# Low parts of two output-projection chunks moved from VectorE to GpSimd, and a planner that counts on later first loads

## The chip, the cores and the metric

The kernel runs on one core of one Trainium2 chip. The metric is device time in microseconds (us) of one execution; the time before is the median of three. The engines are TensorE (PE; PEld is its weight load), VectorE (DVE), ScalarE (ACT) and GpSimd (POOL). SyncE (SP) issues every DMA of the kernel, in one queue. SBUF is the memory on the chip that all engines read, PSUM the accumulators (eight banks) that TensorE writes.

## What is computed

Two independent halves share one output of 2048 rows: 448 columns from a Fourier mixing (A) and 448 from attention with 16 heads of width 28 (B).

```python
a = einsum("bsd,ed->bse", x, dft_hid_re); b = einsum("bsd,ed->bse", x, dft_hid_im)
A = einsum("ts,bse->bte", dft_seq_re, a) - einsum("ts,bse->bte", dft_seq_im, b)
q, k, v = split_heads(x @ wqkv)                      # S = 2048, D = 448, H = 16
p = softmax(einsum("bhqd,bhkd->bhqk", q, k) * Dh ** -0.5)
B = merge_heads(einsum("bhqk,bhkd->bhqd", p, v)) @ wo
out = concatenate([A, B], axis=-1)
```

All is float32. TensorE multiplies in a reduced form of it, so most operands are split: a high part (a ScalarE copy into that form) and a low part (the original less the high part, a subtraction on VectorE or GpSimd), and a product takes three matmuls: high by high, low by high, high by low.

## The kernel before

**Work and its order.** Every operation is a task with a key (a due time), the engines that may run it, an estimated duration and the tiles it uses. `Schedule.run` plays the program through once with these estimates and emits each engine's instructions in the order that comes out. On the chip that order is fixed: each engine and the sync queue takes its own list strictly in turn, and waits at an instruction until what it reads is there and what it overwrites has been read. For a load the planner counts a landing time (L274), which for loads planned between T_IN - 6 = 14 us and 45 us has 1.5 us on top.

**The attention.** A unit is one head by 512 queries. In most units ("kept", `unit_kept`) TensorE makes the scores once (L809), ScalarE copies them from PSUM to SBUF (L416), and VectorE takes the running maximum (L816, L819). A chain of small VectorE operations turns that into a shift per query (L824 to L842), which ends in a PSUM bank; ScalarE copies it to SBUF (`mb`, L844). Then eight pairs of tiles are shifted (L859, 128x1024: on VectorE with the shift read from PSUM, or on GpSimd with the shift from `mb`; the first three pairs of a unit, and all pairs of the last units, may go to either) and exponentiated on ScalarE (L863). Eighteen units ("twice", `unit_twice`) make the scores a second time instead, with the maximum as two rows of the product (L755, L759, then L787), and ScalarE exponentiates straight from PSUM (L791). Both end in products with V in two groups of sixteen matmul records (L736), accumulated in one bank and copied to a tile `ou` (L416 on ScalarE or L418 on VectorE).

**Normalising.** `out_of` folds `ou` (L878), copies the result to SBUF (L880), and takes the sums through DRAM: a store-and-load into `sm` (L883), a reciprocal on VectorE (L884), a store to `rd` (L885), a load that spreads it (L889), a product on GpSimd (L892) and the store of the attention output to `ond` (L895). For the last two heads this is done per chunk of 512 queries.

**The output projection**, at the end, per chunk `n` of 512 queries in the order 0, 1, 3, 2: four loads of the attention output from `ond` (L952, and L957 twice for the last 64 rows, which hang on the last two heads). For each half chunk (256 columns) and each of the four pieces `k`, ScalarE makes the high part in a tile of the `k` pool (L970), and a subtraction the low part. The subtraction is recorded in the helper `sub`, so it shows as L412: 128x256, for the last piece 64x256; eight for a chunk. With `early` it goes to VectorE, otherwise to GpSimd. Then TensorE makes four output tiles a chunk, eleven matmuls each (L988), which are copied (L416 or L418) and stored (L995).

**The Fourier half and the weights** fill TensorE's gaps all through: L548 (projections of Q and K, V, and the hidden transform) and L663 (the sequence transform) with pieces of weights that are loaded (L516), copied to a high part on ScalarE (L517) and subtracted to a low part on GpSimd (L523, L532). Q and K go to a DRAM tensor `qkd` (L593, L594), V to `vd` (L620), and come back per head and unit (L690 and L691 for `k` and `q`, L708 for `v`).

Of the kernel before, what the change touches and what calls it, by code (L numbers as in the profile page):

```python
# [39 lines left out]
GV = 8  # L40

TWICE = [(1, 3) if h in (4, 10) else (1,) for h in range(H - 2)] + [(3,), (3,)]
OUT_DVE = True

LAST = (0, 1, 3, 2)

# [124 lines left out]
class Schedule:  # L171
# [34 lines left out]
    def run(self):  # L206
# [10 lines left out]
        while True:  # L217
            for e in self.ENGINES:
                if not idle[e]:
                    continue  # L220
                aside, pick, first = [], None, None
                if e == "SP" and len(landed) >= LANES and landed[-LANES] > now + 1e-9:
                    heapq.heappush(events, (landed[-LANES], 2, count, "tick", None))
                    continue
                heap = self.ready[e]
                before = now - (AHEAD if e == "PE" else 0.0) + 1e-9
                while heap:
                    item = heapq.heappop(heap)
                    t = item[2]
                    if t.n in done:  # L230
                        continue
                    wants = {}
                    for s in t.use:
                        if s.i is None:
                            wants.setdefault(s.pool, []).append(s)
                    if t.since > before or any(not p.can_take(w, before, now) for p, w in wants.items()) or any(
                            x.lock > now + 1e-9 for x in t.lock):
                        aside.append(item)
                        continue
                    if e == "PE" and mode == 1 and t.mode == 0 and pick is None:  # L240
                        if not any(x[2].mode == 1 and x[2].n not in done for x in heap):
                            pick = t
                            break
                        first = first or item
                        aside.append(item)
                        continue
                    pick = t
                    break
                if pick is None and first:
                    pick = first[2]  # L250
                    aside.remove(first)
                for item in aside:
                    heapq.heappush(heap, item)
                if pick is None:
                    continue
                t = pick
                done.add(t.n)
                for s in t.use:
                    if s.i is None:
                        s.pool.take(s)  # L260
                dur = t.engs[e]
                if e == "PE":
                    if t.mode > mode:
                        dur += PE_TURN
                    mode = t.mode
                lat = t.lat
                if e == "SP":

                    at = now
                    for size, extra in t.dmas:  # L270
                        if len(landed) >= LANES:
                            at = max(at, landed[-LANES])
                        flow = max(flow, at + 0.4) + size / (FLOW if now > T_IN else FLOW_IN)
                        landed.append(max(at + 1.35 + size / 170 + extra + (1.5 if T_IN - 6 < now < 45 else 0.0), flow + 1.1))  # L274
                        at += 0.38
                    dur = at - now
                    lat = max(landed[-len(t.dmas):]) - at + 0.1
                t.emit(e)
                count += 1
                idle[e] = False  # L280
                for x in t.lock:
                    x.lock = now + dur + 0.05
                heapq.heappush(events, (now + dur, 0, t.n, "free", (e, t)))
                heapq.heappush(events, (now + dur + t.own, 1, t.n, "own", (e, t)))
                heapq.heappush(events, (now + dur + lat, 1, t.n, "seen", (e, t)))
                if t.lock:
                    heapq.heappush(events, (now + dur + 0.06, 2, t.n, "tick", None))
# [31 lines left out]
def tile_kernel(ctx, tc, xa, wre, wim, wd, xb, wqkv, wo, out):  # L319
# [624 lines left out]
    for n, c in enumerate(LAST):  # L944
# [15 lines left out]
        for i in range(2):  # L960
            x = [kt_s.slot() for _ in range(4)]
            ready = []
            for k in range(4):
                raw, ld = raws[k]
                src = lambda raw=raw, i=i: raw.t[:, i * HF:(i + 1) * HF]
                xh, xl = x[k // 2], x[2 + k // 2]
                hi = lambda xh=xh, k=k: xh.t[:, k % 2 * HF:(k % 2 + 1) * HF]
                lo = lambda xl=xl, k=k: xl.t[:, k % 2 * HF:(k % 2 + 1) * HF]
                key = T_OUT + n + i / 2
                a = act(key, lambda hi=hi, src=src: nc.scalar.activation(hi(), src(), AF.Copy), 0.3, deps=[ld], use=[raw.pair, xh])  # L970
                if k < 3:
                    b = sub(key, lo, src, lambda hi=hi: f32(hi()), d=0.35 if OUT_DVE else 0.65, early=OUT_DVE, deps=[a], use=[raw.pair, xh, xl])
                else:
                    b = sub(key, lambda hi=hi: hi()[64:], lambda src=src: src()[64:], lambda hi=hi: f32(hi())[64:], d=0.35 if OUT_DVE else 0.65, early=OUT_DVE,
                            deps=[a], use=[raw.pair, xh, xl])
                ready += [a, b]
            for t in range(2):
                o = bank_s.slot()

                def cols(k, x=x, t=t):  # L980
                    return lambda: x[k // 2].t[:, k % 2 * HF + t * P:k % 2 * HF + (t + 1) * P]
                seq = products(cols, lambda k, cols=cols: cols(4 + k), lambda cols=cols: cols(3),
                               lambda k: (lambda: w_out.h[:, k]), lambda k: (lambda: w_out.l[:, k]))
                key = T_OUT + 5 + (n * 4 + i * 2 + t) * 2.3

                def emit(e, seq=seq, o=o):
                    for n, (x, w) in enumerate(seq):
                        nc.tensor.matmul(o.t[:, :D], x(), w(), start=(n == 0), stop=(n == 10))  # L988
                m = pe(key, emit, n=11, d=M448, deps=[*ready, *wo_ready], use=[o, *x])
                pair = kept_s.slot()  # L990
                oo = Half(pair, 0)
                e = sch.add({"ACT": 0.43, "DVE": 0.53}, key, lambda e, o=o, oo=oo: copy_of(e, oo.t[:, :D], o.t[:, :D]),
                            deps=[m], use=[o, pair])
                r0 = c * CH + i * HF + t * P
                dma(key, lambda oo=oo, r0=r0: nc.sync.dma_start(out[r0:r0 + P, D:], oo.t[:, :D]), deps=[e], use=[pair])  # L995
# [38 lines left out]
```

## Time and profile before

| what | value |
|---|---|
| median of three runs | 1165.0 us (1163.15 to 1166.09) |
| the profiled execution's own time | 1165.2 us |
| its span, first to last instruction | 1163.4 us, mean granted TensorE clock 0.997 |
| VectorE's low parts of the output projection, 128x256 | 24, mean 0.75 us |
| the same, 64x256 | 8, mean 0.55 us |
| GpSimd's idle time by the waits | 85.6 us for `mb` (L844), 81.1 us for weights (L517) |

How to read the rows: a group row of the waits has engine, what is written, line, then whom it waited for, the total in us, how often, and the longest. A stretch row has its bounds and width, then each engine's busy time with the instructions in brackets, the granted clock (1.00 is full), the share of the DMA engines that is busy, and GB/s. A timeline row has start, duration, engine, line, operation, output<-inputs, shapes, how many in a row, and in square brackets the idle time before and what ended it. SPq rows are issues of DMAs on the sync queue. Matmuls overlap, so the step from one start to the next tells TensorE's pace, not the duration of one row.

### The profile page before, as it was taken

The numbers are of one execution on the slowest core, as the hardware profiler recorded it, in microseconds if no ns is written. First come the engines' busy times: TensorE is split into PE (matmuls) and PEld (weight loads), VectorE is DVE, ScalarE is ACT, GpSimd is POOL, SyncE is SP. The second block draws the span as 40 slices with busy tenths as digits, with TensorE's granted clock in tenths as the row PEclk, the third lists the DMA queues.
The fourth block names the chain that finished last, engine by engine and source line by source line (L and its number), as shares of the span: only waits on it lengthen the run. The fifth ranks groups of instructions, "written<-read, shape, count | busy, mean of one in ns | idle before, by whom it ended". The sixth has DMA issues, their size and how long they took to land.

```text
span 1163.4 us, 19480 instructions
## 1 busy us (share of the span) xinstructions
PE 1142.1 (98%) x6076; PEld 775.1 (67%) x6076; DVE 1012.8 (87%) x1800; ACT 1044.8 (90%) x1782; POOL 917.5 (79%) x534
## 2 busy tenths in 40 slices
PE   8999999999999999999999999999999999999898
PEld 6875666566666666676767576667666666766577
DVE  6599989999999899899989898999998999999832
ACT  5269999999999999999999999999998999999742
POOL 3048887899988889889888999899887998988410
PEclk9999999999999999999999999999999999999999
DMA  8883353222323232332333332222323332323452
GB/s 267 189 175 134 113 177 122 75 86 82 103 69 87 69 110 84 92 92 89 90 94 102 95 95 72 79 80 89 113 93 99 104 120 91 95 64 105 151 158 101
DMA packets 111840, 125.17 MB, mean 108 GB/s; under 512 B 49348, under 2 KB 63316, under 8 KB 111736
## 3 DMA queue, kind: packets, MB, share of 16 engines
q1 hardware_dynamic: 111736, 123.93, 35.7%
q8 instruction: 48, 0.79, 0.3%
q14 instruction: 56, 0.46, 0.1%
HBM read 89.99 MB, written 33.76 MB: 106 GB/s over the span
## 4 chain that ended last, share of the span: by engine, by line
PE 84%; DVE 6%; ACT 4%; issue 2%; DMA 2%; POOL 1%; SPq 1%; DVEq 0%; ACTq 0%; POOLq 0%
PE bank L663 27%; PE bank L736 18%; PE bank L809 14%; PE bank L548 9%; PE bank L787 6%; PE bank L755 5%; PE bank L988 3%; DVE rm L819 2%; ACT kept L416 2%; PE bank L878 1%; POOL kept L859 1%; ACT kept L863 1%; DVE k L412 1%; DMA kept<-wqkv 1%; DVE mx L759 1%
## 5 line engine op out<-in xcount | busy, mean ns | idle before, releaser
L859 POOL TENSOR_TENSOR kept<-kept,mb 128x1024 f32<-128x1024 f32 x269 | 641.1, 2405 | 88.4 <-ACT mb L844 85.6
L819 DVE TENSOR_TENSOR rm<-bank,rm 128x512 f32<-128x512 f32 x644 | 441.1, 685 | 53.4 <-ACT kept L416 20.0
L416 ACT ACTIVATE kept<-bank 128x512 f32<-128x512 f32 (+1 forms) x696 | 410.7, 658 | 59.7 <-PE bank L809 34.6
L863 ACT ACTIVATE kept<-kept 128x1024 f32<-128x1024 f32 x354 | 385.1, 1133 | 12.8 <-DVE kept L859 8.7
L663 PE MATMUL bank<-big,whi 128*128 128x448 f32 x1024 | 324.4, 368 | 0.3 <-DVE big L644 0.3
L809 PE MATMUL bank<-q,k 84*128 84x512 f32 x736 | 286.4, 414 | 4.5 <-ACT kept L416 2.7
L523 POOL TENSOR_TENSOR wlo<-wraw,whi 128x512 fp32r<-128x512 f32 (+1 forms) x166 | 204.9, 1236 | 106.8 <-ACT whi L517 81.1
L736 PE MATMUL bank<-kept,v 128*32 128x512 f32 x1940 | 244.2, 598 | 4.3 <-ACT kept L791 4.1
L663 PEld LDWEIGHTS bank<-big,whi 128*128 128x128 f32 x1024 | 194.2, 190 | 31.7 <-issue 5.2
L759 DVE TENSOR_REDUCE mx<-bank 128x1 f32<-128x512 f32 x288 | 194.8, 680 | 12.1 <-PE bank L755 11.0
L809 PEld LDWEIGHTS bank<-q,k 84*128 84x128 f32 x736 | 134.9, 189 | 99.5 <-DVE rm L819 15.3
L663 PE MATMUL bank<-big,wlo 128*128 128x448 f32 x512 | 188.5, 368 | 0.0
L791 ACT ACTIVATE kept<-bank 128x512 f32<-128x512 f32 x262 | 169.3, 669 | 5.3 <-PE bank L787 5.1
L736 PEld LDWEIGHTS bank<-kept,v 128*32 128x32 f32 x1940 | 56.2, 109 | 122.8 <-issue 108.8
L517 ACT ACTIVATE whi<-wraw 128x512 fp32r<-128x512 f32 x167 | 117.4, 704 | 3.2 <-DMA wraw<-wqkv 2.3
L755 PE MATMUL bank<-k,q 84*128 84x512 f32 x288 | 117.8, 412 | 2.2 <-DMA q<-qkd 1.8
L787 PE MATMUL bank<-q,k 86*128 86x512 f32 x288 | 115.8, 409 | 0.7 <-DMA q<-nmd 0.4
L663 PEld LDWEIGHTS bank<-big,wlo 128*128 128x128 f32 x512 | 97.2, 190 | 13.8 <-issue 0.8
L859 DVE TENSOR_TENSOR kept<-kept,bank 128x1024 f32<-128x1024 f32 x85 | 102.3, 1209 | 2.5 <-ACT mb L844 2.1
L548 PE MATMUL bank<-wd,whi 128*128 128x448 f32 x256 | 80.0, 371 | 0.1
L755 PEld LDWEIGHTS bank<-k,q 84*128 84x128 f32 x288 | 54.2, 189 | 31.1 <-issue 6.0
L548 PE MATMUL bank<-big,whi 128*128 128x512 f32 x196 | 70.1, 402 | 3.4 <-DVE big L412 1.3
(82 smaller groups left out, 1094.0 us busy)
## 6 DMA issues: line engine op xcount, KB each, us to landing
wraw<-wre SPq DMA_DIRECT2D x64, 256.0 KB
wraw<-wim SPq DMA_DIRECT2D x64, 256.0 KB
qkd<-wd SPq DMA_DIRECT2D x32, 256.0 KB
wraw<-xa SPq DMA_DIRECT2D x32, 256.0 KB
k<-qkd SPq DMA_DIRECT2D x64, 112.0 KB
q<-qkd SPq DMA_DIRECT2D x64, 112.0 KB
out<-kept SPq DMA_DIRECT2D x32, 224.0 KB
qkd<-kept SPq DMA_DIRECT2D x24, 256.0 KB
```

Source lines behind the costliest of these rows:

```text
L416: nc.scalar.activation(dst, src, AF.Copy)
L523: b = sch.add(e, at, lambda g: eng[g].tensor_tensor(self.lo.t[:, :n], raw.t[:, :n], f32(self.hi.t)[:, :n], op=ALU.subtract), deps=[a], acq ...
L548: nc.tensor.matmul(o.t[:, :cols], w(), x(), start=(i == 0), stop=(i == n - 1))
L663: nc.tensor.matmul(o.t[:, :D], a.t[:, k, :], b[:, q * 4 + k, :], start=(q == 0 and k == 0 and j == 0), stop=(q == 3 and k == 3 and j == 2))
L736: nc.tensor.matmul(o.t[j * VW:(j + 1) * VW, :], VT[h].t[:, kt // 4, j, :], pairs[i // 2].t[:, i % 2, :], start=(kt < 4), stop=(kt >= NT - 4))
L755: m = pe(key, lambda e, o=o, kc=kc, qt=qt: nc.tensor.matmul(o.t, q.t[:KR, qt * P:(qt + 1) * P], KT[h][kc].t[:KR, :], start=True, stop=True ...
L759: ms.append(dve(key - 20, lambda o=o, kc=kc, qt=qt: nc.vector.tensor_reduce(mx.t[:, qt, kc:kc + 1], o.t, axis=AX.X, op=ALU.max), deps=[m], ...
L787: m = pe(key, lambda e, o=o, kt=kt: nc.tensor.matmul(o.t, KT[h][kt // 4].t[:KR + 2, kt % 4 * P:(kt % 4 + 1) * P], q.t[:KR + 2, :], start=T ...
L809: m = pe(key, lambda e, o=o, kt=kt: nc.tensor.matmul(o.t, KT[h][kt // 4].t[:KR, kt % 4 * P:(kt % 4 + 1) * P], q.t[:KR, :], start=True, sto ...
L819: prev = dve(key - 20, lambda o=o: nc.vector.tensor_tensor(rm.t, o.t, rm.t, op=ALU.max), deps=[m, prev], use=[rm, o], lock=[o], own=RAW)
L859: eng[e].tensor_tensor(s.t, s.t, over_pair(pm.t if e == "DVE" else mb.t), op=ALU.add)
L863: es.append(act(key, lambda s=s: nc.scalar.activation(s.t, s.t, AF.Exp, scale=SCALE), 0.96, deps=[sh], use=[s]))
```

## The change

Two constants of the plan and one threshold. `n` is the place of the chunk in the output projection, so with `OUT_DVE = 2` chunks 0 and 1 have their subtractions on GpSimd (planned at 0.65 us instead of 0.35), chunks 2 and 3 on VectorE as before. The planned landing of loads between 14 and 42 us (45 before) has 3.0 us on top instead of 1.5. No operation is added or removed; the orders change where the planner's times do.

```diff
-OUT_DVE = True
+OUT_DVE = 2
...
-    landed.append(max(at + 1.35 + size / 170 + extra + (1.5 if T_IN - 6 < now < 45 else 0.0), flow + 1.1))
+    landed.append(max(at + 1.35 + size / 170 + extra + (3.0 if T_IN - 6 < now < 42 else 0.0), flow + 1.1))
...
 if k < 3:
-    b = sub(key, lo, src, lambda hi=hi: f32(hi()), d=0.35 if OUT_DVE else 0.65, early=OUT_DVE, deps=[a], use=[raw.pair, xh, xl])
+    b = sub(key, lo, src, lambda hi=hi: f32(hi()), d=0.35 if n >= OUT_DVE else 0.65, early=n >= OUT_DVE, deps=[a], use=[raw.pair, xh, xl])
 else:
...
```

The last piece's 64 rows (the `else` branch) are changed in the same way. What moves in the orders, buffer numbers left out. At the start: TensorE's first L755 comes five L548 later; VectorE makes one more copy of V (L616) before the first L759; on the sync queue one Q/K store pair's first half and one V store go ahead of the first `k` load, and two weight loads (L516) go from before the first twice unit's `q` load to behind the eighth `k` load. At the end: the sixteen subtractions stand in GpSimd's list, between the last L523 and L892; of the last kept unit's eight shifts seven are VectorE's and one GpSimd's (six and two before); one `ou` copy is ScalarE's; one L663 goes ahead of a fold; and some stores and loads of the normalising change places on the sync queue.

More of the change, by code (lines that the diff above doesn't have):

```diff
@@ L971, in tile_kernel @@
                 if k < 3:
-                    b = sub(key, lo, src, lambda hi=hi: f32(hi()), d=0.35 if OUT_DVE else 0.65, early=OUT_DVE, deps=[a], use=[raw.pair, xh, xl])
+                    b = sub(key, lo, src, lambda hi=hi: f32(hi()), d=0.35 if n >= OUT_DVE else 0.65, early=n >= OUT_DVE, deps=[a], use=[raw.pair, xh, xl])
                 else:
-                    b = sub(key, lambda hi=hi: hi()[64:], lambda src=src: src()[64:], lambda hi=hi: f32(hi())[64:], d=0.35 if OUT_DVE else 0.65, early=OUT_DVE,
+                    b = sub(key, lambda hi=hi: hi()[64:], lambda src=src: src()[64:], lambda hi=hi: f32(hi())[64:], d=0.35 if n >= OUT_DVE else 0.65, early=n >= OUT_DVE,
                             deps=[a], use=[raw.pair, xh, xl])
```

## The prediction

> **What bounds the kernel now.** I read the busy shares on the page first, then who TensorE waited for, then stretches of the span, and last the timelines of the two places where TensorE stood still.
>
> ```profile
> PE 1142.1 (98%) x6076; PEld 775.1 (67%) x6076; DVE 1012.8 (87%) x1800; ACT 1044.8 (90%) x1782; POOL 917.5 (79%) x534
> ```
> ```profile
> PE bank L736 <- ACT kept L791: 4.1, 1, 4.1
> PE bank L809 <- ACT kept L416: 2.7, 3, 1.5
> PE bank L755 <- DMA q<-qkd: 1.8, 1, 1.8
> ```
> ```profile
> 300.00:600.00 300.00, 299.98 (x1660) 203.61 (x1656) 277.15 (x484) 293.01 (x495) 265.67 (x140) 1.00 0.29 90
> ```
> ```profile
> 1099.10:1107.20 8.10, 8.02 (x32) 3.33 (x33) 8.01 (x11) 7.26 (x13) 1.28 (x1) 0.79 0.85 240
> 1107.20:1159.60 52.40, 52.33 (x260) 45.23 (x259) 15.35 (x35) 18.81 (x42) 6.37 (x5) 1.00 0.40 132
> ```
>
> TensorE is the pace: 98% busy, and 299.98 of 300 us in the middle. So only two kinds of thing pay: TensorE instructions saved (none here, both programs have the same ones) and TensorE's stops. The longest, 4.1 us, stands near the end, and one of 1.8 us near the start; the change touches both places. In the stretches the columns after the width are PE, PEld, DVE, ACT, POOL, then the granted clock. From 1107.2 us to 1159.6 TensorE works without a break (52.33 of 52.40), so what it loses before that is lost to the end.
>
> **The end: what stops TensorE.** The timelines of TensorE, VectorE, GpSimd and ScalarE:
>
> ```profile
> 1088.04 1.92 PE L736 MATMUL bank<-kept,v 128*32 128x512 f32 x16
> ...
> 1093.20 1.91 PE L736 MATMUL bank<-kept,v 128*32 128x512 f32 x12
> 1099.18 2.40 PE L736 MATMUL bank<-kept,v 128*32 128x512 f32 x4 [4.08 <-ACT kept L791]
> 1101.52 0.74 PE L663 MATMUL bank<-big,whi 128*128 128x448 f32 x1
> ...
> 1107.20 0.67 PE L663 MATMUL bank<-big,whi 128*128 128x448 f32 x2
> ...
> 1110.35 2.40 PE L988 MATMUL bank<-wd,k 128*128 128x448 f32 x11
> ```
> ```profile
> 1088.21 0.73 DVE L842 STREAM_TRANSPOSE bank<-bank 128x512 f32<-128x512 f32 x1
> 1088.85 7.57 DVE L412 TENSOR_TENSOR k<-kept,k 128x256 fp32r<-128x256 f32 x2
> 1096.35 4.60 DVE L859 TENSOR_TENSOR kept<-kept,bank 128x1024 f32<-128x1024 f32 x4
> ```
> ```profile
> 1090.01 1.48 POOL L892 TENSOR_TENSOR kept<-kept 64x512 f32<-64x512 f32 x1
> 1091.44 4.70 POOL L859 TENSOR_TENSOR kept<-kept,mb 128x1024 f32<-128x1024 f32 x2
> ```
> ```profile
> 1090.11 0.60 ACT L416 ACTIVATE ou<-bank 128x512 f32<-128x512 f32 x1
> 1097.59 1.06 ACT L863 ACTIVATE kept<-kept 128x1024 f32<-128x1024 f32 x1 [6.88 <-DVE kept L859]
> 1098.55 1.06 ACT L791 ACTIVATE kept<-bank 128x512 f32<-128x512 f32 x2
> ```
>
> Follow it backwards. TensorE (1099.18) waits for the exponentials of L791. They stand in ScalarE's queue behind an L863, which waits 6.88 us for VectorE's shift (L859). That one stands behind two low parts of the output projection (L412, 128x256), which take 7.57 us together. They end at 1096.42, just after GpSimd's products and shifts are through (1091.44 + 4.70 = 1096.14). A VectorE subtraction with both operands in SBUF thus seems to stand still while GpSimd works on SBUF.
>
> What it costs TensorE: sixteen L736 take 1.92 us (the group at 1088.04), so those begun at 1093.20 would be over at 1095.12. The next instruction starts at 1101.52: **6.4 us** lost. From there to 1107.20, 5.68 us, the granted clock is 0.79 in the mean, and 0.21 of 5.68 is **1.2 us** more. Together 7.6 us.
>
> **The change at the end.** Sixteen subtractions, eight each of the first two chunks, go from VectorE to GpSimd. In the order of the changed program VectorE goes from the transpose L842 straight to seven shifts (six before), GpSimd keeps one shift (two before), and one copy of `ou` goes from VectorE to ScalarE. Their prices:
>
> ```profile
> 1065.09 2.41 POOL L859 TENSOR_TENSOR kept<-kept,mb 128x1024 f32<-128x1024 f32 x1 [0.32 <-ACT mb L844]
> ```
> ```profile
> 1065.40 1.20 DVE L859 TENSOR_TENSOR kept<-kept,bank 128x1024 f32<-128x1024 f32 x1
> ```
> ```profile
> L523 POOL TENSOR_TENSOR wlo<-wraw,whi 128x512 fp32r<-128x512 f32 x128 | 165.8, 1296 | 73.5 <-ACT whi L517 55.8 <-PE bank L809 9.6 <-ACT n L767 3.0
> ...
> L528 POOL TENSOR_TENSOR whi<-wraw,whi 64x128 fp32r<-64x128 f32 x32 | 14.6, 457 | 2.5
> ```
>
> A shift on VectorE reads one operand from PSUM and takes 1.15 us in a row (four in 4.60); beside a GpSimd shift it still takes 1.20. So nothing holds VectorE up. The shifts run from 1088.9 (L842's end) and end at 1090.1, 1091.2, 1092.4, 1093.5 and so on to 1097.0. ScalarE (0.96 for a shift's exponential, 1097.59 to 1098.55; two L791 in 1.06) is free after its copy at 1090.7: first L863 to 1091.7, both L791 done at **1092.7**, before TensorE's group at 1093.20 begins. The stop is gone. What is late next: the fold waits for ScalarE's copy of `ou`, done about 1097 (behind three more L863, a piece of the weights and its own 0.6), while TensorE has run its sixteen L736 and nine L663 (0.21 each, fifteen between 1107.20 and 1110.35) at 1097.0: about 0.1 us. The next group of L736 needs the first half's L863, done before that copy: no wait.
>
> GpSimd's price for 256 columns is not in the trace: above 0.46 (L528, 128 columns), below 1.30 (L523, 512). I take 0.74, on the line between the two. Sixteen are 12 us, on an engine that is busy for 6.37 of the 52.4 us after 1107.2. In its queue: the first two end at 1089.4, then a weight piece, the product L892, its shift (to 1094.3) and the rest of the first chunk, for whose last pieces it waits on ScalarE's copies (L970, to 1099). The four subtractions that TensorE's first output tile needs are done at about 1099.5; TensorE comes to that tile at 1110.35 less 7.5, or 1102.8. At 1.30 each it would be 1102: still in time. The next load of the attention output (L952) overwrites the tile that the slow subtraction reads, so it goes out some 7 us earlier as well, and with it all that stands behind it on the sync queue. **End: 7.6 less 0.1 = 7.5 us**; bounds 4 (something given back) to 8.
>
> **The change at the start.** The planner's landing time for loads between 14 and 42 us grows by 1.5 us; that moves a few entries of the orders.
>
> ```profile
> 39.29 0.40 PE L809 MATMUL bank<-q,k 84*128 84x512 f32 x1
> 41.45 0.47 PE L755 MATMUL bank<-k,q 84*128 84x512 f32 x1 [1.75 <-DMA q<-qkd]
> ```
> ```profile
> 30.87 1.48 SPq L516 DMA_DIRECT2D wraw<-wqkv  x1
> ...
> 33.12 2.10 SPq L516 DMA_DIRECT2D wraw<-wqkv  x1
> ...
> 38.24 0.63 SPq L691 DMA_DIRECT2D q<-qkd  x1
> ```
> ```profile
> 87.17 0.69 ACT L517 ACTIVATE whi<-wraw 128x512 fp32r<-128x512 f32 x1
> ```
>
> In the changed order five L548 (128x448 like L663, so 0.21 each) stand ahead of the first L755: it comes up at 39.7 + 1.0 = 40.7 instead of 39.7. And two weight loads of 256 KB (30.87 and 33.12, 3.6 us of the sync queue) move behind the `q` load of 38.24, by a good 20 us; the next piece to be copied after those of the first 32 us is that at 87.17, so it costs nothing. The `q` that landed at 41.4 lands between 37.8 (the whole queue time) and 39.6 (half of it): before 40.7 either way, and the stop of 1.75 is gone. **The start: 1.75 us**; if `q` landed no earlier at all, the five matmuls alone would save 1.0. The two stores and the copy of V that now go ahead of the first `k` load delay it by some 2 us, with 12 us before its use at 39.29. VectorE does one V copy earlier than the first L759; its wait for L755 hid that.
>
> From there to 1088 us the orders of TensorE, ScalarE, VectorE and GpSimd are the same once the buffers' numbers are left out (the sync queue's from about 62 us). So the 1.75 us is carried through: the other engines are fed by TensorE there.
>
> **The sum.** The profiled execution took 1165.2 us (span 1163.4 and 1.8 around it), 0.2 above the median of 1165.0. 1165.2 - 7.5 - 1.75 = 1155.95; less the 0.2, **1155.8 us**.
>
> **Rivals.** *Start absorbed:* a later stop that ends at a fixed time (the 2.7 us of L809 waiting for ScalarE's copies) takes the 1.75 back: 1157.5. Against it: those waits are for engines that TensorE itself feeds.
>
> *Given back on the last chunks' way through DRAM.* The normaliser of the third chunk (L883, L885, L889, then L892 on GpSimd) keeps its place among waits for later copies in the sync queue, and L892 now stands behind fourteen of the moved subtractions:
>
> ```profile
> 1121.41 1.27 POOL L892 TENSOR_TENSOR kept<-kept 64x512 f32<-64x512 f32 x1
> ```
> ```profile
> 1132.05 0.42 ACT L970 ACTIVATE k<-kept 128x256 fp32r<-128x256 f32 x1 [0.20 <-DMA kept<-ond]
> ```
> ```profile
> 1136.66 2.62 PE L988 MATMUL bank<-wd,k 128*128 128x448 f32 x12
> ```
>
> In the changed sync order its reload L889 stands behind the store of the third output tile. That tile is through at 1102.8 + three tiles of 2.25 + twelve L663 + a group of L736, or 1114.0; 0.8 for its copy, 0.9 for the issue and 2.5 for the landing (as `q`: 38.87 to 41.4) give L892 at 1118.2, only 3.2 us earlier, while TensorE is 7.5 earlier. Before, it took 10.6 us from L892's start to the copy L970 behind the reload (1132.05), queue waits included, and 1 more to the low part: 1129.9. TensorE comes to the third chunk one tile after the row at 1136.66 (2.3 us), less 7.5: at 1131.5. That is 1.6 us to spare, so nothing; were L892 4.6 us later than I count, 3 us are lost: 1159. The Trainium skill (TensorE: Matmul & The Clock Gate, "What's actually happening") has the clock halved by an idle window of about 3.4 us, until TensorE has worked as long again. Half speed for 3.4 of 8.1 us is a mean of 0.79, as the row has it; by that page 3 us lost in shorter stops would stay 3.
>
> *Port exchanged, not freed.* The moved subtractions hold GpSimd's side and VectorE's shifts wait for them as the subtraction did: the stop at 1095 stays and only the start gains, 1163.3. Against it stands the VectorE shift of 1.20 us beside GpSimd's 2.41. The Trainium skill (Perfetto Trace Analysis, "Optimizing Scalar/DVE Operations") warns that shifting work between these two may not help, since they share an SBUF read port; by that page this rival would hold.
>
> *Slower.* The same way through L892, if GpSimd's queue holds it far longer: from 1119.8 on every us is TensorE's, and past 9.25 us more (L892 after 1129) the kernel is slower than before; at 1133, 1169. The fourteen subtractions ahead of it would have to take 0.8 us more each than the 0.74 that I count, beyond GpSimd's 1.30 for twice the width. What speaks for it: they wait for ScalarE's copies, and these for TensorE to let go of the tiles.
>
> **Numbers.** Both gains 0.65 (1154 to 1157.5), start absorbed 0.11, given back 0.10, port exchanged 0.06, slower 0.08. Range 1153.8 to 1160.3, which takes in the first three. A measurement tells about 0.3% (3.5 us) from no change: faster 0.86, the same 0.06, slower 0.08.
>
> **What would show it.** Right: no TensorE wait of over 0.5 us for L791; VectorE's first shift within 1 us of L842's end; L412 on GpSimd near 0.74; the first L755 without a wait for its `q`; clock 1.00 after 1090. Wrong: TensorE waiting at L988 for a GpSimd L412 or for a load from `ond`, a VectorE shift of over 2 us, or a new wait for loads before 90 us.

## The result and the profile after

The changed kernel takes **1154.15 us** (median of 6 runs, 1152.55 to 1157.88), against 1164.24 for the kernel before in the same set (6 runs, 1159.68 to 1166.09). The ratio is 0.9919, with a 95% interval of 0.9896 to 0.9942: 9.4 us off, between 6.7 and 12.1. (The ratio is not that of the two medians, which lie 10.1 us apart.) Forecast were 1155.8 us and a gain of 9.25. The profiled execution of the changed kernel took 1153.29 us, with a span of 1151.5.

The busy line of the page after, then its longest waits of TensorE (engine, what is written, line, whom it waited for; total us, times, longest):

```profile
PE 1136.9 (99%) x6076; PEld 771.0 (67%) x6076; DVE 998.5 (87%) x1784; ACT 1045.6 (91%) x1783; POOL 926.7 (80%) x549
```
```profile
PE bank L809 <- ACT kept L416: 2.7, 3, 1.6
PE bank L904 <- POOL ident masks.py:199: 1.4, 1, 1.4
PE bank L548 <- ACT big L483: 1.1, 1, 1.1
PE bank L809 <- DVE bank L842: 0.7, 2, 0.6
```

Both stops on which the prediction rested are off the list: no 4.1 us for L791, no 1.8 us for `q`. The first line here stood second before, unchanged at 2.7 us.

**The end.** TensorE's timeline after: the group of sixteen L736 that ran into the stop before (its start was 1093.20 there), and the first output tile:

```profile
1088.75 1.92 PE L736 MATMUL bank<-kept,v 128*32 128x512 f32 x16
...
1098.30 2.41 PE L988 MATMUL bank<-wd,k 128*128 128x448 f32 x11
```

From that group to the first L988 it is 9.55 us; before it was 1110.35 - 1093.20 = 17.15. So the end gave **7.6 us**. This distance is the yardstick for all runs below, since it leaves out what happened earlier in an execution. VectorE, GpSimd and ScalarE in the same place:

```profile
1083.76 0.73 DVE L842 STREAM_TRANSPOSE bank<-bank 128x512 f32<-128x512 f32 x1
1085.15 8.01 DVE L859 TENSOR_TENSOR kept<-kept,bank 128x1024 f32<-128x1024 f32 x7 [0.66 <-ACT mb L844]
```
```profile
1083.55 1.44 POOL L412 TENSOR_TENSOR k<-kept,k 128x256 fp32r<-128x256 f32 x2
1084.93 1.30 POOL L523 TENSOR_TENSOR wlo<-wraw,whi 128x512 fp32r<-128x512 f32 x1
1086.18 1.29 POOL L892 TENSOR_TENSOR kept<-kept 64x512 f32<-64x512 f32 x1
1087.43 2.42 POOL L859 TENSOR_TENSOR kept<-kept,mb 128x1024 f32<-128x1024 f32 x1
```
```profile
1087.37 1.07 ACT L791 ACTIVATE kept<-bank 128x512 f32<-128x512 f32 x2
```

VectorE goes from the transpose to seven shifts in a row, 8.01 us, beside a GpSimd that is busy all the time, and ScalarE has both L791 done at 1088.4, before TensorE's group starts. The stretches show TensorE without a gap at full clock (the column before the DMA share), where before it had 0.79 over 8.1 us:

```profile
1080.00:1090.00 10.00, 10.00 (x62) 6.62 (x64) 8.89 (x16) 9.62 (x19) 7.70 (x7) 1.00 0.72 228
1090.00:1100.00 10.00, 10.00 (x60) 6.60 (x53) 3.78 (x4) 8.93 (x14) 7.74 (x9) 1.00 0.89 281
```

**The start.** TensorE's timeline after:

```profile
37.99 0.40 PE L809 MATMUL bank<-q,k 84*128 84x512 f32 x1
38.23 1.18 PE L548 MATMUL bank<-wd,big 128*128 128x448 f32 x5
39.25 0.40 PE L755 MATMUL bank<-k,q 84*128 84x512 f32 x1
39.49 0.57 PE L548 MATMUL bank<-wd,big 128*128 128x448 f32 x2
39.89 0.40 PE L809 MATMUL bank<-q,k 84*128 84x512 f32 x1
```

and before, the two rows behind its L809 of 39.29 and its L755 of 41.45:

```profile
41.76 1.59 PE L548 MATMUL bank<-wd,big 128*128 128x448 f32 x7
43.19 0.40 PE L809 MATMUL bank<-q,k 84*128 84x512 f32 x1
```

Five of the seven L548 now stand ahead of L755, and L755 has no wait. From L809 to L809, with the same L755 and seven L548 between them, it was 43.19 - 39.29 = 3.90 us and is 39.89 - 37.99 = 1.90: **2.0 us**. The second half of its `q` load also goes out 3.3 us earlier (38.24 before), as the prediction had it:

```profile
34.90 0.42 SPq L691 DMA_DIRECT2D q<-qkd  x1
```

**The rest of the pair.** The two spans differ by 11.9 us; 7.6 and 2.0 are 9.6 of it. The first of these L809 already starts 1.3 us earlier (37.99 against 39.29), from unequal waits before it, and some 1.3 us come from the clock near 704 us (last section). I put neither down to the change: two profiles of one and the same kernel below (start only) have this L809 at 39.41 and at 38.17 us, and kernels with the new start have clocks of 0.79 as well as 1.00 near 704 us.

### The profile page after: what moved, and what is told of

Same layout as the page of the kernel before. It is cut to its first block, busy times and chain, and to the rows that moved or that the text cites. A ratio compares the mean times of both kernels' runs of the same rounds, so it can differ in the third digit from the quotient of the medians.

```text
span 1151.5 us, 19491 instructions
## 1 busy us (share of the span) xinstructions
PE 1136.9 (99%) x6076; PEld 771.0 (67%) x6076; DVE 998.5 (87%) x1784; ACT 1045.6 (91%) x1783; POOL 926.7 (80%) x549
## 4 chain that ended last, share of the span: by engine, by line
PE 82%; ACT 7%; DVE 6%; issue 2%; POOL 2%; DMA 1%; SPq 0%; DVEq 0%; ACTq 0%; POOLq 0%
PE bank L663 27%; PE bank L736 17%; PE bank L809 14%; PE bank L548 9%; PE bank L787 5%; PE bank L755 5%; PE bank L988 3%; ACT kept L416 3%; DVE rm L819 3%; ACT kept L863 2%; POOL kept L859 2%; PE bank L878 1%; ACT kept L791 1%; DVE mx L759 1%; DMA kept<-wqkv 1%
## 5 line engine op out<-in xcount | busy, mean ns | idle before, releaser
L416 ACT ACTIVATE kept<-bank 128x512 f32<-128x512 f32 (+1 forms) x696 | 411.3, 659 | 54.1 <-PE bank L809 31.6
L663 PE MATMUL bank<-big,whi 128*128 128x448 f32 x1024 | 324.2, 368 | 0.3 <-DVE big L644 0.3
L809 PE MATMUL bank<-q,k 84*128 84x512 f32 x736 | 286.2, 414 | 4.6 <-ACT kept L416 2.7
L523 POOL TENSOR_TENSOR wlo<-wraw,whi 128x512 fp32r<-128x512 f32 (+1 forms) x166 | 205.0, 1236 | 85.3 <-ACT whi L517 58.7
L736 PE MATMUL bank<-kept,v 128*32 128x512 f32 x1940 | 241.8, 597 | 0.2
L663 PEld LDWEIGHTS bank<-big,whi 128*128 128x128 f32 x1024 | 193.6, 189 | 31.1 <-issue 4.2
L759 DVE TENSOR_REDUCE mx<-bank 128x1 f32<-128x512 f32 x288 | 194.8, 680 | 8.7 <-PE bank L755 7.7
L809 PEld LDWEIGHTS bank<-q,k 84*128 84x128 f32 x736 | 134.5, 188 | 100.3 <-DVE rm L819 15.3
L663 PE MATMUL bank<-big,wlo 128*128 128x448 f32 x512 | 188.1, 367 | 0.0
L791 ACT ACTIVATE kept<-bank 128x512 f32<-128x512 f32 x262 | 169.6, 670 | 4.9 <-PE bank L787 4.7
L736 PEld LDWEIGHTS bank<-kept,v 128*32 128x32 f32 x1940 | 55.5, 109 | 117.7 <-issue 108.5
L755 PE MATMUL bank<-k,q 84*128 84x512 f32 x288 | 117.3, 410 | 0.5
L663 PEld LDWEIGHTS bank<-big,wlo 128*128 128x128 f32 x512 | 96.9, 189 | 14.1 <-issue 0.8
L548 PE MATMUL bank<-wd,whi 128*128 128x448 f32 x256 | 79.1, 367 | 0.1
L755 PEld LDWEIGHTS bank<-k,q 84*128 84x128 f32 x288 | 54.0, 188 | 29.2 <-issue 5.9
L787 PEld LDWEIGHTS bank<-q,k 86*128 86x128 f32 x288 | 53.9, 188 | 28.5 <-DVE rm L819 7.3
```

Of the source, the lines that this page charges most:

```text
L416: nc.scalar.activation(dst, src, AF.Copy)
L523: b = sch.add(e, at, lambda g: eng[g].tensor_tensor(self.lo.t[:, :n], raw.t[:, :n], f32(self.hi.t)[:, :n], op=ALU.subtract), deps=[a], acq ...
L548: nc.tensor.matmul(o.t[:, :cols], w(), x(), start=(i == 0), stop=(i == n - 1))
L663: nc.tensor.matmul(o.t[:, :D], a.t[:, k, :], b[:, q * 4 + k, :], start=(q == 0 and k == 0 and j == 0), stop=(q == 3 and k == 3 and j == 2))
L736: nc.tensor.matmul(o.t[j * VW:(j + 1) * VW, :], VT[h].t[:, kt // 4, j, :], pairs[i // 2].t[:, i % 2, :], start=(kt < 4), stop=(kt >= NT - 4))
L755: m = pe(key, lambda e, o=o, kc=kc, qt=qt: nc.tensor.matmul(o.t, q.t[:KR, qt * P:(qt + 1) * P], KT[h][kc].t[:KR, :], start=True, stop=True ...
```

## Experiments

**1 and 2: each half alone.** The landing constant put back; then only the landing constant:

```diff
 # end only, from the changed kernel
-... (3.0 if T_IN - 6 < now < 42 else 0.0)
+... (1.5 if T_IN - 6 < now < 45 else 0.0)
 # start only, from the kernel before
-... (1.5 if T_IN - 6 < now < 45 else 0.0)
+... (3.0 if T_IN - 6 < now < 42 else 0.0)
```

> Only the move of the eight subtractions of the first two output chunks to GpSimd; the planned landing of the first loads stays as before. The port theory (VectorE's two-SBUF subtraction of the first chunk stood behind three GpSimd instructions, the last unit's shifts queued behind it, TensorE waited 6.4 us for them and then ran 8 us at a clock of 0.79): 7.5 us off before (6.5 to 8.5), no TensorE wait for L791 over 0.5 us, clock 1.00 after 1090, first L755 still waiting 1.8 us for q. Rival, the part of the pair's 11.9 us that neither 7.4 at the end nor 1.75 at the start holds (2.7 us in small steps) belongs to this part: 10 us off.

> Only the planned landing time of the first loads (3.0 us later, until 42 us); the subtractions stay on VectorE. The q theory (the first scores of the twice-computed head waited 1.75 us for q, and five L548 matmuls planned ahead of them take that place): 1.75 us off before (1.0 to 2.3), the 6.4 us wait for L791 and the 0.79 clock stay. Rival, the small steps between 289 and 880 us come from the start's other order: 3 to 4.4 us off. Rival, absorbed by a later wait: within 0.5 us of before.

The end alone: 1158.26 us against 1164.76, ratio 0.9944 (0.9928 to 0.9959), 6.5 us off (4.8 to 8.4). Its first L755 still waits 1.6 us for `q`, and the distance at the end is 9.55 us, as in the full change. The start alone: 1160.08, ratio 0.9961 (0.9944 to 0.9978), 4.5 us off (2.6 to 6.5). The step at the start is 2.0 us as forecast, but the total is more than the 1.75 that I expected, and its end, which has before's instructions in before's order on TensorE, ScalarE, VectorE and GpSimd, does not look like before's. TensorE there:

```profile
1091.07 1.92 PE L736 MATMUL bank<-kept,v 128*32 128x512 f32 x16
1098.07 1.09 PE L736 MATMUL bank<-kept,v 128*32 128x512 f32 x3
1098.93 3.39 PE L736 MATMUL bank<-kept,v 128*32 128x512 f32 x13
1105.39 2.41 PE L988 MATMUL bank<-wd,k 128*128 128x448 f32 x11
```

14.32 us instead of 17.15. What differs is found on VectorE. The view of one tile gives the durations in ns (min/median/max) of the subtractions that start in a window; for the two behind the transpose L842 in before, and for three in the start-only kernel:

```profile
L412 DVE TENSOR_TENSOR k<-kept,k x2: 1486/3825/6164, 1088.8 to 1090.3; 128x256 fp32r<-128x256 f32 x2
```
```profile
L412 DVE TENSOR_TENSOR k<-kept,k x3: 401/1505/2947, 1086.7 to 1093.0; 128x256 fp32r<-128x256 f32 x3
```

In before one of the two takes 6.16 us; in the start-only kernel none does. So the stall has a long form and a short one. (The third subtraction, of 2.95 us, is taken up in experiment 11.)

**3: before once more**, to see whether the length is fixed.

> Before, unchanged, profiled a second time. If the length of the stall depends on how the two engines' requests fall (the start-only kernel had 1.50 us in the place of 6.16 with the same instructions in the same order), the second subtraction behind L842 may take 1.5, 2.9 or 6.2 us here, and the stop of TensorE at L791 be shorter or as long; if it is fixed by the order, 6.2 us and 4.1 us of wait again. The 1.8 us wait for q and the clock of 0.98 between 700 and 800 us should be there again, if they belong to the kernel and not to the execution.

The same two subtractions in this second profile, the start of the first and of GpSimd's L523 beside it, and TensorE's group:

```profile
L412 DVE TENSOR_TENSOR k<-kept,k x2: 401/954/1508, 1088.2 to 1088.6; 128x256 fp32r<-128x256 f32 x2
```
```profile
1088.24 1.83 DVE L412 TENSOR_TENSOR k<-kept,k 128x256 fp32r<-128x256 f32 x2
```
```profile
1088.26 1.53 POOL L523 TENSOR_TENSOR wlo<-wraw,whi 128x512 fp32r<-128x512 f32 x1 [0.78 <-ACT whi L517]
```
```profile
1092.59 1.92 PE L736 MATMUL bank<-kept,v 128*32 128x512 f32 x16
...
1105.44 2.40 PE L988 MATMUL bank<-wd,k 128*128 128x448 f32 x11
```

The same kernel, 1160.3 us, 12.85 us at the end instead of 17.15, with 1.9 us of wait for `q` (1.8 in the first profile). The stall is a race. Here the first subtraction starts 0.02 us ahead of L523 and takes 0.40; GpSimd waits (1.53). GpSimd's L523 in before's first profile:

```profile
1088.77 1.28 POOL L523 TENSOR_TENSOR wlo<-wraw,whi 128x512 fp32r<-128x512 f32 x1 [0.77 <-ACT whi L517]
```

There the subtraction (1088.85) came 0.08 us behind L523 and waited itself; the second then came up beside L892, and the long form followed. The start times alone do not decide within some hundredths of a us: in the start-only kernel's profile the subtraction starts 0.02 us behind L523 (1086.72 and 1086.70) and still goes first (0.40 us, L523 1.57). In the profiles in which it lost, it was 0.06 to 0.12 us behind.

The 1.5 us between this 12.85 and the start-only kernel's 14.32 go with the clock. Both have the short form and a stop of 2.3 us at the fold, but the mean granted clock over the distance was 1.00 here and 0.88 there.

**4: the start-only kernel once more**, because its 4.5 us had asked whether its order makes the short form the rule.

> The start-only kernel, unchanged, profiled a second time. Its first look had the short wait at the end (1.50 us in the place of 6.16 for the second subtraction, 14.3 us from the last long L736 group to the first L988, against 17.15 in before), and its median lies 4.5 us under before's where the start alone is worth 2.0. If its other start makes the short wait the rule, this look has it again (12.8 to 14.4 us); if it is chance from one execution to the next, as in the two looks at before (17.15 and 12.85), either may come, and a long one (about 17 us) refutes the first. The step at the start is 2.0 us in both cases.

It was long: 6.16 us again, 1107.89 - 1090.30 = 17.59 us at the end, the step at the start again 2.0. So the start-only order does not make the short form the rule: one kernel has either.

**5: the subtractions back on VectorE, but behind its shifts.** This keeps the work on VectorE and changes only its place:

```diff
-OUT_DVE = 2
+OUT_DVE = 0
...
-             deps=[ld, t, cs[2 * i], cs[2 * i + 1]], ...)
+             deps=[ld, t, cs[2 * i], cs[2 * i + 1]], ...); last_shifts.extend([sh] * (u == units[-1]))
...
-    b = sub(key, lo, src, ..., deps=[a], ...)
+    b = sub(key, lo, src, ..., deps=[a, *last_shifts * (n < 2)], ...)
```

> After, but the eight subtractions are back on VectorE and are made to depend on all of the last unit's shifts, so VectorE runs them behind its shifts and no two-SBUF subtraction stands ahead of a shift. GpSimd keeps two of the shifts, as in before. The port theory: it was the place in VectorE's queue that cost, not which engine does the work: same time as after within 1.5 us, no wait for L791 over 0.7 us; the first L988 needs four subtractions of 0.41 to 0.45 us behind the last VectorE shift at about 1093 to 1095, that is 1097, before TensorE reaches it at 1098. Rival, VectorE was simply short of time in this stretch and only work taken off it helps: 3 to 7 us of the gain are lost, with L791 or L988 waiting for DVE L412.

1154.37 us, ratio 0.9911 (0.9896 to 0.9925): the whole gain. The end is 9.55 us, to the hundredth that of the full change. VectorE there:

```profile
1086.35 6.88 DVE L859 TENSOR_TENSOR kept<-kept,bank 128x1024 f32<-128x1024 f32 x6 [0.67 <-ACT mb L844]
1093.14 3.90 DVE L412 TENSOR_TENSOR k<-kept,k 128x256 fp32r<-128x256 f32 x8
```

The eight subtractions end at 1097.0 and the first L988 starts at 1099.48. VectorE was not short of time; a slow instruction stood ahead of one that TensorE waited for.

**6 and 7: how many chunks.** `OUT_DVE` at 4 (all four chunks on GpSimd) and at 1 (the first alone):

> After, with the subtractions of all four output chunks on GpSimd instead of the first two. The port theory: the last two chunks' subtractions stand beside no shift and TensorE has no wait there, so same as after within 1 us; GpSimd's 0.73 us for VectorE's 0.41 shows at most in the last chunk's first L988 (four in a row 2.9 us against 1.7), up to 1.3 us slower than after. Rival, every subtraction on VectorE costs by the port it takes from GpSimd: 1 to 3 us faster than after.

> After, with only the first chunk's eight subtractions on GpSimd; the second chunk's are back on VectorE, where their place is behind the last unit's shifts. The port theory: the second chunk's subtractions never stood ahead of a shift that TensorE waited for, so all of the end gain belongs to the first chunk: same as after within 1 us (about 10 us under before). Rival, half of the gain belongs to each chunk: 3 to 5 us slower than after.

All four: 1155.98 us, ratio 0.9921 (0.9905 to 0.9938). The first alone: 1155.26, ratio 0.9930 (0.9901 to 0.9958). Both have 9.55 us at the end, and cannot be told from the change. Of the sixteen moved subtractions the first chunk's eight carry it, as far as the end shows it; the others neither cost nor gain.

**8: two SBUF operands for the shifts.** If the port is the cause, VectorE's shifts must stall as soon as they read `mb` in SBUF instead of the PSUM bank:

```diff
-... over_pair(pm.t if e == "DVE" else mb.t)
+... over_pair(pm.t if e == "DVE" and u != units[-1] else mb.t)
```

> After, but the last unit's shifts on VectorE read their second operand from its copy mb in SBUF (as GpSimd's shifts do) instead of the PSUM bank; nothing else, and the order on every engine, is changed. So VectorE's shifts have both operands in SBUF. The port theory: they now collide with GpSimd's L892, L859 and L412, between 1086 and 1093: the first shifts end 2.5 to 6 us later, TensorE waits 2 to 6 us for L791, and runs at a lower clock for 8 us behind a wait of over 3.4 us: 3 to 8 us slower than after. Rival, no port is shared and what ended the stall was only the shorter queue: within 0.7 us of after, shifts still 1.13 to 1.2 us each.

1159.62 us, ratio to before 0.9951 (0.9929 to 0.9972), where the change has 0.9919. The end takes 12.80 us instead of 9.55. The seven shifts, which take 1.21 to 1.22 us each after the change, here (ns, min/median/max):

```profile
L859 DVE TENSOR_TENSOR kept<-kept,mb x7: 1214/1759/4658, 1087.9 to 1101.3; 128x1024 f32<-128x1024 f32 x7
```

Same order, same engine, same size; only where one operand lies is changed, and 3.25 us of the 7.6 are given back. I had expected the wait at L791; it appeared as 2.2 us at the fold (L878), behind the copy of `ou`.

**9: the port by itself.**

> A kernel that leaves the whole computation out (its output is zeros): six stages, each started by ScalarE for both engines. 1: VectorE alone, eight 128x256 two-SBUF subtractions. 2: GpSimd four 128x1024 shifts back to back, VectorE the eight subtractions. 3: GpSimd the shifts, VectorE four shifts with one operand in PSUM. 4: GpSimd eight 128x256 subtractions, VectorE eight. 5: GpSimd the shifts, VectorE eight 128x256 copies of one SBUF operand. 6: GpSimd the shifts alone, then VectorE its four shifts alone. The port theory: stage 1 0.41 us each, stage 2 at least one subtraction of over 2 us; if VectorE gets the port between two GpSimd instructions, none over 2.5 us, and if it doesn't, one of 9 to 10 us, as the 6.16 us in before spans three; stage 3 as in stage 6 (1.13 and 2.42); stage 4 about 0.75 each where they alternate. Rival, no shared port: stage 2 like stage 1, 0.41 each.

The subtractions alone (L76), beside four shifts (L82), beside eight subtractions of GpSimd (L94), copies of one SBUF operand beside shifts (L100); then the shifts with an operand in PSUM beside GpSimd (L88) and alone (L107); one row each, VectorE, ns:

```profile
L76 DVE TENSOR_TENSOR vc<-va,vb x8: 424/426/426, 11.2 to 14.4; 128x256 f32<-128x256 f32 x8
```
```profile
L82 DVE TENSOR_TENSOR vc<-va,vb x8: 424/1435/2608, 16.9 to 28.4; 128x256 f32<-128x256 f32 x8
```
```profile
L94 DVE TENSOR_TENSOR vc<-va,vb x8: 425/828/829, 40.9 to 46.5; 128x256 f32<-128x256 f32 x8
```
```profile
L100 DVE COPY vc<-va x8: 293/1302/2479, 49.4 to 60.0; 128x256 f32<-128x256 f32 x8
```
```profile
L88 DVE TENSOR_TENSOR vs<-vs,bank x4: 1220/1220/1221, 31.0 to 34.8; 128x1024 f32<-128x1024 f32 x4
```
```profile
L107 DVE TENSOR_TENSOR vs<-vs,bank x4: 1220/1221/1222, 72.3 to 76.0; 128x1024 f32<-128x1024 f32 x4
```

With an operand in PSUM: 1.22 us either way, so no contention. With both in SBUF: four of the eight wait for one whole GpSimd shift each, and none longer than 2.61 us. The two engines take turns. The Trainium skill (SBUF — State Buffer, "Who interferes with whom") says that the shared port pair is held as an exclusive lock for the whole instruction, and that a VectorE instruction with two SBUF inputs contends with a GpSimd one that reads SBUF; by that rule these rows are as they should be. But turns do not give 6.16 us.

**10 and 11: what takes VectorE's turn.** First before's own row of GpSimd instructions beside the subtractions, then pairs of them:

> A kernel that leaves the whole computation out (its output is zeros). The run before gave VectorE the port once between any two of four GpSimd shifts (2.45 us a subtraction), while before's profile has one subtraction of 6.16 us across three GpSimd instructions. Here GpSimd runs before's own row, with its shapes: one L523 (128x512 subtraction, fp32r), one L892 (64x512), two shifts of 128x1024, while VectorE runs four 128x256 subtractions with fp32r output, in four stages in which VectorE starts 0, 0.2, 0.6 and 1.0 us later; then four shifts, five L892 and five L523 alone, each beside six subtractions. Theory A, VectorE loses its turn behind certain instructions (the L892 of 64 rows and what follows, or fp32r): a subtraction of 3.6 us or more in the first four stages, and one of the last three stages shows which. Theory B, it is a race that depends on when the request comes: long ones in some of the four stages alone. Theory C, the turn is never lost here: every subtraction under 2.6 us, and what made before's last 6.16 us isn't the port's order alone.

> A kernel that leaves the whole computation out (its output is zeros), to find which GpSimd instruction takes VectorE's turn. The run before: in a row of equal instructions VectorE got the port behind each (1.48 or 2.56 us a subtraction), and in the row L523, L892, shift, shift it got it behind L523 and then not again until the row's end (6.07 us). Six stages, each with six 128x256 subtractions on VectorE beside a row of four on GpSimd: 1: L892 (64 rows), three shifts; 2: L523, three shifts; 3: a shift, three L523; 4: a shift, three 128x256 subtractions; 5: the L892 with 128 rows, three shifts; 6: L892, three additions of the same size as the shifts, without the operand that is read twice. Theory A, it is the 64 rows: long ones (8.5 us, across all four) in stages 1 and 6 only. Theory B, a longer instruction behind a shorter one takes the turn: 1, 2, 5 and 6. Theory C, any change of instruction takes it: in all six. Theory D, the operand that is read twice: 1, 2 and 5. In the other stages every subtraction stays under 2.7 us.

In the row L523, L892, shift, shift the long one came in three of four stages, at 6.07 us; in the remaining one VectorE was through before GpSimd began. In rows of equal instructions it never came. The pairs decide. First the row of the 64-row product and three shifts; second, the same with the product over 128 rows; third, the 64-row product and three additions with no operand read twice:

```profile
L92 DVE TENSOR_TENSOR kl<-raw,kh x6: 411/412/8366, 14.4 to 24.0; 128x256 fp32r<-128x256 f32 x6
```
```profile
L92 DVE TENSOR_TENSOR kl<-raw,kh x6: 413/2016/2556, 54.2 to 63.4; 128x256 fp32r<-128x256 f32 x6
```
```profile
L92 DVE TENSOR_TENSOR kl<-raw,kh x6: 411/416/8367, 66.0 to 75.7; 128x256 fp32r<-128x256 f32 x6
```

One subtraction of 8.37 us across all four GpSimd instructions where the first has 64 rows, and none over 2.56 in the four stages without such a product. That is theory A of the expectation; longer behind shorter (B), any change of instruction (C) and the operand read twice (D) fall. A row of 64-row products alone (in the run before this one) gave turns again, at most 1.48 us. So it is a 64-row instruction followed by 128-row ones that takes the turn, in these rows until GpSimd's row ends. The 2.95 us of experiment 2 fit this: that subtraction came up beside the second shift behind L892 and waited through the L523 behind it too (2.96 us in the second profile of before).

The end of the row is not the whole rule, though. In experiment 8 VectorE's second shift waited through L892 and the GpSimd shift behind it (1089.99 to 1094.65, the 4.66 us above), but then went ahead of GpSimd's L412, which came up without a gap and took 1.72 us instead of 0.74:

```profile
1091.19 2.37 POOL L859 TENSOR_TENSOR kept<-kept,mb 128x1024 f32<-128x1024 f32 x1
1093.53 1.72 POOL L412 TENSOR_TENSOR k<-kept,k 128x256 fp32r<-128x256 f32 x1
```

What gives the turn back, and why 64 rows take it, no run shows.

**12: the same cure in the kernel before.** Only the product L892 is changed; the upper 64 rows are multiplied for nothing:

```diff
-nc.gpsimd.tensor_tensor(osb.t[:n * VW], osb.t[:n * VW], sbc.t[:n * VW], op=ALU.mult)
+nc.gpsimd.tensor_tensor(osb.t, osb.t, sbc.t, op=ALU.mult)
```

> Before, with one edit: the normaliser's multiplication L892 of the last four groups runs over 128 rows instead of 64 (the other 64 rows are multiplied for nothing and used by nobody). The order on every engine is before's. Theory, the GpSimd instruction of 64 rows is what takes VectorE's turn at the port until GpSimd's row of instructions ends: the subtraction that took 6.16 us in before's profile now waits for one GpSimd instruction at most (1.5 to 2.7 us), TensorE's wait at the last unit ends 2 to 4 us earlier, and the median falls by 1 to 4 us, with no change to the start (less than the full 4.3 us, as some executions of before have the short wait already). Rival, the rows don't matter here: 6 us subtractions still occur and the time is before's within 0.8 us.

The two subtractions, and GpSimd's start beside the first (VectorE's is 1091.46):

```profile
L412 DVE TENSOR_TENSOR k<-kept,k x2: 1509/1510/1511, 1091.5 to 1092.9; 128x256 fp32r<-128x256 f32 x2
```
```profile
1091.40 1.28 POOL L523 TENSOR_TENSOR wlo<-wraw,whi 128x512 fp32r<-128x512 f32 x1 [0.78 <-ACT whi L517]
1092.65 1.47 POOL L892 TENSOR_TENSOR kept<-kept 128x512 f32<-128x512 f32 x1
```

Here the first subtraction loses the race as in before (0.06 us behind L523), and the second still takes 1.51 us, not 6.16. The end is 1108.36 - 1095.80 = 12.56 us. The median is 1161.26 against 1163.43, ratio 0.9977 (0.9959 to 0.9996): 2.7 us off by the ratio (0.5 to 4.8), 2.2 by the medians. The gain is barely clear of the noise, so the duration of the second subtraction is the stronger sign.

The end in all profiles, each the start of the first L988 less that of the L736 group:

| kernel | us | kernel | us |
|---|---|---|---|
| before | 17.15 | after | 9.55 |
| before, second profile | 12.85 | end only | 9.55 |
| start only | 14.32 | behind the shifts | 9.55 |
| start only, second profile | 17.59 | all four chunks | 9.55 |
| before, L892 with 128 rows | 12.56 | first chunk | 9.55 |
| | | after, shifts from `mb` | 12.80 |

No run gave a version faster than the changed kernel and the one with the subtractions behind the shifts, which cannot be told apart.

## Why the prediction was right

- **The end, 7.5 us.** The profiles give 7.6, and the steps on the way hold: no stop for L791; L412 on GpSimd at 0.74 us; VectorE's shifts unhindered beside GpSimd; clock 1.00. Two details of the changed kernel were off: the first shift started 0.66 us late, because it waits for ScalarE's copy `mb` though it reads the bank, and the fold did not wait 0.1. Neither cost anything. The cause named, a subtraction with both operands in SBUF standing still while GpSimd works, is shown by experiments 8 and 9.
- **A term of the end that was misread:** the 1.2 us for the clock. The prediction takes the mean of 0.79, which belongs to 1099.10 to 1107.20, for the 5.68 us from 1101.52 on. That part alone has 0.91, and 0.09 of 5.68 is 0.5 us. Most of the rest was a wait at the fold, whose weight load waited for VectorE's copy of `ou`. The total holds, since the change removed this wait too:

```profile
1101.52:1107.20 5.68, 5.68 (x29) 2.95 (x29) 5.59 (x8) 4.84 (x9) 0.92 (x1) 0.91 0.85 234
```
```profile
PEld bank L878 <- DVE ou L418: 0.6, 1, 0.6
```

- **What that step left out** is that before's profile was one of two cases. Of four profiles with this order (before and start only, twice each) two had the long form. In the short form each of the first two subtractions waits for one GpSimd instruction at most, not for three; the 6.16 us needed a lost race (by 0.08 us in before's profile) and the 64 rows of L892. Against the second profile of before the end is worth 12.85 - 9.55 = 3.3 us, not 7.6. The gain of a typical execution lies between, and the end-only kernel puts it at 6.5 (4.8 to 8.4).
- **The start, 1.75 us.** It is 2.0 in the pair. The distance from L809 to L809 is 1.90 us in all seven profiles with the new start (the changed kernel, start only twice, experiments 5 to 8). With the old start it varies with the wait for `q`: 3.90 and 4.06 in the two profiles of before, 3.61 in experiment 12, and 4.86 in the end-only kernel, where the clock behind the stop was 0.57 from 40.32 to 43.15. So the same step is worth 1.7 to 3.0 us, by the execution. The wait column undersizes the stop: it counts from the modelled end of L809 (39.29 + 0.40), while the next matmul starts 0.24 us after an L809 (37.99 to 38.23 after). From 39.53 to 41.45 are 1.92, and the step behind L755 was 0.07 longer than 0.24 as well.
- **The sum.** 9.6 by the two places in the profiles, 9.4 (6.7 to 12.1) by the timed runs. That the medians meet the profile so well is partly luck: a profile of before with the short stall would have led the same working to some 5 us. The clock helped as well: its mean over the six timed runs of the changed kernel was 0.9993, over those of experiments 6 and 7, with the same 9.55 us at the end, 0.9977 and 0.9974, which is some 2 us of an execution.
- **The rivals.** Start absorbed: the 2.0 us stay to the end. Given back through L892: it starts at 1114.25, which is 1118.7 on before's clock (4.45 us earlier at 1088), against 1118.2 counted, and TensorE waits nowhere at L988. Port exchanged: the PSUM operand keeps VectorE's shifts free of it; with the operand moved to SBUF this rival comes true in part. The Trainium skill's warning against shifting work between these two engines (Perfetto Trace Analysis, "Optimizing Scalar/DVE Operations") did not come true here: the shifts that TensorE waits for read one operand from PSUM, with 1.22 us alone and beside GpSimd. Slower: L892 was not held.
- **Still open:** the start-only kernel's 4.5 us (2.6 to 6.5), of which the step at the start explains 2.0. The clocks of the timed runs go most of the way for the rest: the mean over its twelve runs is 0.9978, over before's seventeen in the same set 0.9959. What is missing to full clock is then 2.6 us of an execution against 4.7, an estimate from these means, so 2.1 us go with the clock. Whether the new start keeps the clock up (a stop for `q` can cost clock, as in the end-only kernel) or chance did, the runs do not show.

## What to carry to other kernels

Look at what a slow instruction stands ahead of before moving its work: here the same subtractions on the same engine, behind the shifts in its queue, gave the whole gain. A VectorE operation with both operands in SBUF beside a busy GpSimd has no fixed price (0.40 to 6.16 us here for the same subtraction), so its duration in one profile is a draw, and a forecast that removes it should rest on a second execution or give both ends. Let one operand come from PSUM where an engine's queue matters to TensorE: such shifts took 1.22 us alone and beside GpSimd.

## What the runs showed of the hardware

- **The port's turn can be lost.** A waiting VectorE subtraction gets through between two GpSimd instructions (2.61 us at most beside shifts), but after a GpSimd instruction of 64 rows followed by ones of 128 rows it waited to the end of the row where the two engines ran alone: 6.07 us across three instructions and 8.37 across four, counting the one of 64 rows. In experiment 8 the turn came back after one shift (4.66 us for a VectorE shift).
- **A copy waits as well.** A VectorE copy of 128x256 from SBUF to SBUF takes 0.29 us alone and up to 2.48 beside GpSimd's shifts (L100 above).
- **The same stop, two clocks.** TensorE stops for some 1.5 us near 704 us in all these profiles (the longest of its three waits for L416). The stretch 704 to 712 us in the second profile of before and then in the end-only kernel, which has the same order there:

```profile
704.00:712.00 8.00, 6.47 (x33) 4.36 (x35) 7.56 (x17) 8.00 (x16) 6.90 (x7) 1.00 0.25 69
```
```profile
704.00:712.00 8.00, 6.48 (x23) 5.39 (x23) 7.12 (x16) 7.53 (x15) 6.89 (x7) 0.79 0.25 69
```

The busy time is the same, the clock 1.00 in one and 0.79 in the other, which has done fewer matmuls (23 records against 33). Before's first profile had 0.79 as well, the one of after 1.00: 1.3 us of the pair's difference. A stop of about 1.5 us is thus followed by a lower clock in some executions and not in others, and so is one of 2.3 us (1.00 and 0.88 in experiment 3). The prediction's reckoning that shorter stops cost their own length and no more does not hold in every execution.
